# A gated linear-attention kernel with a feed-forward layer: every GpSimd operation also waits for the last VectorE operation on SBUF ahead of it in the planned order

## The chip, the cores and the metric

One NeuronCore of a Trainium2 chip runs the whole program. The metric is the device time of one execution in microseconds, lower is better. Runs of the kernel before the change: 465.85, 466.42 and 466.65 us, median 466.42.

## The reference

Two stages follow each other. First a stabilised recurrence over 768 steps, for 4 batches and 8 heads with head size 40; then a feed-forward layer whose weights are given in float64.

```python
for t in range(S):                                   # S = 768
    m_new = np.maximum(f_gate[:, :, t] + m, i_gate[:, :, t])
    f_stab = np.exp(f_gate[:, :, t] + m - m_new)
    i_stab = np.exp(i_gate[:, :, t] - m_new)
    C = f_stab * C + i_stab * outer(v_t, k_t)        # 40 x 40 for each head
    n = f_stab * n + i_stab * k_t
    y[:, :, t] = sigmoid(o_gate_t) * (C q_t) / max(abs(n q_t), 1)
x = y.transpose(0, 2, 1, 3).reshape(3072, 320)
h = x @ w_in                                         # 320 x 2048
out = (h * np.clip(h + 3, 0, 6) / 6) @ w_out         # 2048 x 320
```

## The kernel before, in words

The recurrence is cut into chunks of 64 steps. A piece of work is a pair of chunks (128 tokens) of one batch; 24 such pieces are grouped into seven units of 2, 2, 4, 4, 4, 4 and 4 pieces, and the eight heads are worked on in two groups of four ("quads").

For each piece and quad TensorE makes score, state and output products in a PSUM tile `xya` (L479, L489, L506, L512); VectorE and GpSimd mask and weigh (`gw`, L401, L406; keys in `nat`, L370) and carry the state `C` (L443, L452, L455). Per unit and quad the output `on` is gated and divided: L593, L595 and L596 make the divisor `rd`, L597 (step `o1`) multiplies by the gate, L598 (step `o2`) divides. L207 copies 64 columns of `on` to where the third transpose wants them, and L613 transposes `on` on TensorE into `xa`; L621 and L623 split that into two parts `xh` and `xl`.

The feed-forward layer runs at full precision by splitting: each weight slice comes as float64 words (`raw`), ScalarE takes the parts out (L648, L653, L658), VectorE clips, shifts and adds (L663, L664, L669, L674) to a float32 `yi` (first layer) or `vr` (second layer). A high part is cast (L207, `whi`, `vh`) and the low part is the difference (`wlo` L695 for GpSimd, `wtl` L692 and L693 on VectorE, `vl` L710). The first layer is L738 (eight matmuls of a 128-column group, tile `h`); ScalarE's L755 and VectorE's L757 make the gated `g` (`gv` in the first unit), which is split into `gh` (L207) and `gl` (L768, on GpSimd or VectorE), and L784 to L786 (L781 in the first unit) accumulate the second layer in `acc`. Output tiles are copied and stored from the SP queue.

Each step was registered with `add(key, engines, function, after, ...)`. The order of all steps on all engines is the table `ORDER`, written out beforehand: each token holds the number of a step, the letter of the engine that runs it (`d` VectorE, `g` GpSimd, `a` ScalarE, `p` TensorE, `q` the SP queue) and buffer slots. A loop at the end walks through the table and calls the step. The lists `after` serve there only for an assertion that what a step needs stands ahead of it in the table; the waits in the program are made by the tile framework, from who writes and reads which tile. Steps whose entry carries `lock=1` are those that read and write SBUF without PSUM and have some size: L274 to L286, L370, L401, L406, L597, L598, the casts L207 out of SBUF, L663 to L674, the differences L692 to L695, L710 and L768. The small divisor steps L593, L595 and L596 do not carry it.

Of the kernel before, what the change touches and what calls it, by code (L numbers as in the profile page):

```python
# [14 lines left out]
ALU = mybir.AluOpType  # L15
ET = mybir.EngineType

B, H, S, D = 4, 8, 768, 40
# [110 lines left out]
class Ops:  # L129
# [5 lines left out]
    def add(self, key, engs, fn, after=(), get=(), **meta):  # L135
        assert key not in self.at, key
        self.at[key] = len(self.ops)
        self.ops.append((key, engs, fn, list(after), list(get)))
        self.meta[key] = meta
# [3 lines left out]
def mlstm_moe_kernel(ctx: ExitStack, tc: tile.TileContext, ig, fg, qkd, natd, ond, w_in, w_out, ident_d, out, dump=None):  # L143
    nc = tc.nc
# [30 lines left out]
    tiny = cst.tile([128, 1], F32, name="tiny")  # L175
# [14 lines left out]
    T = Ops()  # L190
    add = T.add
# [8 lines left out]
    def E(c):  # L200
        return {"d": nc.vector, "g": nc.gpsimd}[c]
# [28 lines left out]
    def fill(n):  # L230
        for _ in range(n):
            nc.tensor.matmul(pw, ones[:, :128], ones[:, :512], start=True, stop=True)  # L232
# [90 lines left out]
    c0 = 0  # L323
# [246 lines left out]
    for x in NAMES:  # L570
        nm = f"{x[0]}_{x[1]}_{x[2]}"
# [5 lines left out]
    def fin(u, quad, c0, n):  # L577
        task = f"{u}_{quad}"
        nm = f"{task}_{c0}"
        W = 160 * n  # L580

        def hts():
            return V["ht", task][:, c0 : c0 + n]

        def hf():
            return hts().rearrange("p u h e -> p (u h) e")

        def ofs():
            return V["on", u][:, c0 : c0 + n, quad * 160 : quad * 160 + 160].rearrange("p u (h e) -> p u h e", h=4)

        def r1(e):
            rd = V["rd", nm] = at.tile([128, 4 * UM], F32, tag=f"rd{got[f'rd{nm}'][1]}", name=f"rd{nm}")[:, : 4 * n]
            nc.vector.scalar_tensor_tensor(rd, hf()[:, :, D], -1.0, hf()[:, :, D], ALU.mult, ALU.max)  # L593
        add(f"r1{nm}", "d", r1, [f"b2{task}_{c0 + n - 1}"], get=[(f"rd{nm}", ("rd",))], kind="tiny", n=8)
        add(f"r2{nm}", "d", lambda e: nc.vector.tensor_scalar(V["rd", nm], V["rd", nm], 1.0, 2.0, ALU.max, ALU.mult), [f"r1{nm}"], kind="tiny", n=8)  # L595
        add(f"r3{nm}", "d", lambda e: nc.vector.reciprocal(V["rd", nm], V["rd", nm]), [f"r2{nm}"], kind="recip", n=8)  # L596
        add(f"o1{nm}", "d", lambda e: nc.vector.scalar_tensor_tensor(ofs(), ofs(), 1.0, hts()[:, :, :, 0:D], ALU.add, ALU.mult), [f"b2{task}_{c0 + n - 1}", f"tanh{u}"], kind="tt", n=W, lock=1)  # L597
        add(f"o2{nm}", "dg", lambda e: E(e).tensor_tensor(ofs(), ofs(), V["rd", nm].rearrange("p (u h) -> p u h", u=n)[:, :, :, None].broadcast_to([128, n, 4, D]), ALU.mult), [f"o1{nm}", f"r3{nm}"], kind="tt", n=W, lock=1)  # L598
        T.free(f"rd{nm}", [f"o2{nm}"])
        T.free(f"ht{task}", [f"o1{nm}"])  # L600
# [25 lines left out]
    for u in range(NU):  # L626
        for quad in range(2):
            for c0, n in steps(u):
                fin(u, quad, c0, n)
        for f in range(3):  # L630
            for c0, n in steps(u):
                turn(u, f, c0, n)
        T.free(f"x{u}", [f"m1_{u}_{NF-1}"])
# [193 lines left out]
    def name(a):  # L827
        return T.alias.get(a, a)

    done = set()  # L830
    keys = list(T.at)
    for tok in ORDER.split():
        if tok[0] not in "FT":
            i = next(k for k, ch in enumerate(tok) if ch.isalpha())
            chosen[T.ops[int(tok[:i])][0]] = tok[i]
    with tc.manual_schedule(engines={ET.PE, ET.Activation, ET.DVE, ET.Pool, ET.SP}):
        for tok in ORDER.split():
            if tok[0] == "F":
                fill(int(tok[1:] or 1))
                continue  # L840
            if tok[0] == "T":
                nc.scalar.activation(pre, half, AF.Tanh)
                continue
            i = next(k for k, ch in enumerate(tok) if ch.isalpha())
            key, engs, fn, after, get = T.ops[int(tok[:i])]
            e, slots = tok[i], tok[i + 1 :].split("/") if len(tok) > i + 1 else []
            assert e in engs and key not in done and all(name(a) in done for a in after), (key, [a for a in after if name(a) not in done])
            for (who, tags), s in zip([g for g in get if g[0] not in got], slots, strict=True):
                k, n = divmod(int(s), 10)
                assert n < SLOTS[tags[k]], (key, who)  # L850
                got[who] = (tags[k], n)
            fn(e)
            done.add(key)
        assert len(done) == len(T.ops), [k for k in keys if k not in done][:9]

# [66 lines left out]
```

## Time and profile before

| | |
|---|---|
| median of three runs | 466.42 us (465.85 to 466.65) |
| the profiled execution, own time | 464.87 us |
| its span on the engines' clock | 463.2 us |
| mean granted TensorE clock | 0.996 of full speed |
| busy: TensorE, weight load | 97%, 84% of the span |
| busy: VectorE, ScalarE, GpSimd | 65%, 47%, 26% |
| chain that ended last | TensorE 85%, VectorE 9%, ScalarE 2% |

The profiled execution took 464.87 us, 1.55 us less than the median of the runs; its engines' span of 463.2 us leaves 1.67 us around it. Busy shares are means over the whole span. Stages of the program differ, so they are read by stretches of time. A row of a timeline gives start, duration, engine, line, operation and tiles; where the engine was idle ahead of it, the row ends with the idle time and what ended it.

### The profile page before, as it was taken

The page shows a single profiled execution, that of the slowest core. Times are in us where ns is not written, and L with a number is a line of the kernel's source. Part 1 is how long each engine was busy: PE and PEld are TensorE (multiplying, and loading weights), DVE is VectorE, ACT ScalarE, POOL GpSimd, SP SyncE. Part 2 cuts the span into 40 slices and gives each one's busy share as a digit, 9 for nine tenths or more (in the row PEclk, how much of TensorE's full clock was granted, in tenths as well). Part 3 has the DMA queues.
Part 4 walks back from the last instruction along what each step waited for, and adds up shares of the span by engine and source line. Part 5 has one row for each costly group of instructions (what it writes and reads, how often), then busy time and mean ns, then how long its engine had stood idle before and what let it go on. Part 6 is the DMA issues. An engine that isn't in the chain of part 4 may idle for free.

```text
span 463.2 us, 12600 instructions
## 1 busy us (share of the span) xinstructions
PE 449.1 (97%) x5243; PEld 388.3 (84%) x5249; DVE 298.8 (65%) x752; ACT 215.8 (47%) x482; POOL 122.4 (26%) x155
## 2 busy tenths in 40 slices
PE   8879989999999999999999999999999999999997
PEld 4547767899888888988889988988989898989896
DVE  6999999978866376856655763576555646443423
ACT  5788798777343434263343353243551232321231
POOL 3152225265311307502213134132112201020130
PEclk9989999999999999999999999999999999999999
DMA  6998887276304450244421442432322000010001
GB/s 208 281 315 265 234 258 203 59 176 169 94 20 119 119 151 4 78 142 121 115 77 44 131 139 60 108 102 89 101 69 78 1 1 1 16 57 1 1 1 57
DMA packets 24977, 49.38 MB, mean 107 GB/s; under 512 B 2840, under 2 KB 15960, under 8 KB 24920
## 3 DMA queue, kind: packets, MB, share of 16 engines
q1 hardware_dynamic: 24696, 47.89, 35.5%
q8 instruction: 41, 0.67, 0.6%
q10 hardware_dynamic: 224, 0.69, 0.5%
q14 instruction: 16, 0.13, 0.1%
HBM read 44.53 MB, written 4.03 MB: 105 GB/s over the span
## 4 chain that ended last, share of the span: by engine, by line
PE 85%; DVE 9%; ACT 2%; issue 1%; DMA 1%; SPq 0%; DVEq 0%; ACTq 0%
PE h L738 35%; PE acc L784 11%; PE acc L785 11%; PE acc L786 11%; PE xya L506 3%; PE xya L479 3%; PE pw L232 2%; PE xya L489 2%; PE xa L613 2%; PE xya L512 2%; PE acc L781 1%; DVE on L597 1%; DMA st<-in_qk_dram 1%; DVE on L598 1%; DVE gv L757 1%
## 5 line engine op out<-in xcount | busy, mean ns | idle before, releaser
L755 ACT ACTIVATE g<-h,half 128x512 f32<-128x512 f32 (+1 forms) x96 | 61.8, 651 | 128.3 <-PE h L738 92.9
L784 PE MATMUL acc<-vh,gh 128*128 128x320 f32 x352 | 111.5, 317 | 0.0
L757 DVE SCALAR_TENSOR_TENSOR g<-g,h 128x512 f32<-128x512 f32 (+1 forms) x96 | 61.2, 640 | 77.4 <-ACT g L755 77.3
L785 PE MATMUL acc<-vl,gh 128*128 128x320 f32 x352 | 108.6, 309 | 0.0
L786 PE MATMUL acc<-vh,gl 128*128 128x320 f32 x352 | 108.5, 308 | 0.0
L768 POOL TENSOR_TENSOR gl<-g,gh 128x512 fp32r<-128x512 f32 (+1 forms) x40 | 48.7, 1222 | 183.6 <-DVE gh L207 104.2
L738 PE MATMUL h<-xh,whi 128*128 128x512 f32 (+1 forms) x224 | 83.9, 375 | 2.4 <-DVE gv L757 1.7
L738 PE MATMUL h<-xh,wlo 128*128 128x512 f32 (+1 forms) x224 | 80.8, 361 | 0.0
L738 PE MATMUL h<-xl,whi 128*128 128x512 f32 (+1 forms) x224 | 80.5, 360 | 0.0
L784 PEld LDWEIGHTS acc<-vh,gh 128*128 128x128 f32 x352 | 66.0, 188 | 2.5
L785 PEld LDWEIGHTS acc<-vl,gh 128*128 128x128 f32 x352 | 66.1, 188 | 1.8
L786 PEld LDWEIGHTS acc<-vh,gl 128*128 128x128 f32 x352 | 66.0, 188 | 0.0
L738 PEld LDWEIGHTS h<-xh,whi 128*128 128x128 f32 x224 | 42.0, 187 | 11.4 <-DVE gv L757 3.7
L205 ACT CAST gh<-g 128x512 fp32r<-128x512 f32 (+1 forms) x53 | 30.0, 571 | 39.8 <-PE acc L785 19.5
L738 PEld LDWEIGHTS h<-xh,wlo 128*128 128x128 f32 x224 | 42.1, 188 | 6.9
L768 DVE TENSOR_TENSOR gl<-g,gh 128x512 fp32r<-128x512 f32 (+1 forms) x56 | 40.0, 722 | 12.2 <-ACT gh L205 10.9
L738 PEld LDWEIGHTS h<-xl,whi 128*128 128x128 f32 x224 | 42.1, 188 | 4.5
L738 PE MATMUL h<-xl,wtl 128*128 128x512 f32 (+1 forms) x112 | 40.5, 361 | 0.0
L738 PE MATMUL h<-xh,wtl 128*128 128x512 f32 (+1 forms) x112 | 40.2, 359 | 0.0
L419 DVE TENSOR_TENSOR gw<-xya,gw 128x256 f32<-128x256 f32 x48 | 20.0, 416 | 10.7 <-PE xya L489 7.4
L452 DVE SCALAR_TENSOR_TENSOR C<-C,dec,xya 128x42 f32<-128x42 f32 x100 | 20.6, 251 | 9.1 <-PE xya L489 9.0
L207 DVE CAST gh<-g 128x512 fp32r<-128x512 f32 (+1 forms) x43 | 19.3, 451 | 7.5 <-PE acc L785 6.1
(136 smaller groups left out, 683.2 us busy)
## 6 DMA issues: line engine op xcount, KB each, us to landing
st<-in_qk_dram SPq DMA_DIRECT2D x48, 280.0 KB, 4.2
nat<-in_nat_dram SPq DMA_DIRECT2D x48, 206.0 KB, 3.2
rawo<-in_w_out_dram SPq DMA_DIRECT2D x8, 640.0 KB, 7.9
gw<-gsc SPq DMA_DIRECT2D x20, 256.0 KB, 4.3
rawi<-in_w_in_dram SPq DMA_DIRECT2D x7, 640.0 KB, 8.5
out_dram<-ob SPq DMA_DIRECT2D x24, 160.0 KB, 3.0
on<-in_on_dram SPq DMA_DIRECT2D x5, 640.0 KB, 4.9
rawi<-in_w_in_dram ACTq DMA_DIRECT2D x1, 640.0 KB, 4.2
```

The lines of the kernel that those rows point to most:

```text
L205: nc.scalar.copy(dst, src)
L207: E(c).tensor_copy(dst, src)
L419: add(f"fr{nm}", "d", lambda e: nc.vector.tensor_tensor(V["gw", task][:, cp], V["xy", "S", nm][:, :, 0:128].rearrange("p c (j t) -> p j c ...
L452: nc.vector.scalar_tensor_tensor(Cn[:, j], cur[:, j], dc[:, j : j + 1], kv[:, hc, j], ALU.mult, ALU.add)
L479: nc.tensor.matmul(xy[h * Q : h * Q + Q, c, j * Q : j * Q + Q], st[rs, j, h], st[rs, j, 2 + (h != c)], start=True, stop=True)
L738: nc.tensor.matmul(hp[:, :n], w, x[:, :n], start=k == 0, stop=k == len(seq) - 1)
L755: nc.scalar.activation(V["g", nm], V["h", nm][:, :n], AF.Relu, bias=half, scale=1.0 / 6.0)
L757: add(f"gg{nm}", "d", lambda e: nc.vector.scalar_tensor_tensor(V["g", nm], V["g", nm], 1.0, V["h", nm][:, :n], ALU.min, ALU.mult), [f"re{n ...
L768: add(f"gl{nm}", "gd", lambda e: E(e).tensor_sub(V["gl", nm], V["g", nm], V["gh", nm].bitcast(F32)), [f"gh{nm}"], kind="tt", n=n, lock=1)
L784: nc.tensor.matmul(acc, gh[:, ts_], V["VH", f // 4][:, f % 4, :], start=f == 0, stop=False)
L785: nc.tensor.matmul(acc, gh[:, ts_], V["VL", p][:, f % 2, :], start=False, stop=False)
L786: nc.tensor.matmul(acc, gl[:, ts_], V["VH", f // 4][:, f % 4, :], start=False, stop=f == NF - 1)
```

## The change

Two things are edited. In `fin`, two lists `after` now name every step that made a part of `ht`, not only the last one. In the final loop, each GpSimd step gets one more dependency: its first GpSimd instruction also waits for the last instruction of the latest VectorE step with `lock=1` that the table has ahead of it.

```diff
-        add(f"r1{nm}", "d", r1, [f"b2{task}_{c0 + n - 1}"], ...
+        add(f"r1{nm}", "d", r1, [f"b2{task}_{c0 + i}" for i in range(n)], ...
...
+    sync = mybir.DependencyInfo(mybir.DependencyClass.Sync, mybir.DependencyReason.DATA)
+    ahead = None
     for tok in ORDER.split():
...
+            traced = nc.cur_bb.bb.instructions
+            n0 = len(traced)
             fn(e)
+            new = traced[n0:]
+            if e == "g" and ahead is not None:
+                tc.add_manual_dep(next(x for x in new if x.engine == ET.Pool), ahead.name, sync, reason="port")
+            if e == "d" and T.meta[key].get("lock"):
+                ahead = [x for x in new if x.engine == ET.DVE][-1]
             done.add(key)
```

The sequence of instructions on every engine stays as it was; what changes is what GpSimd's instructions wait for. On GpSimd, where units 0 and 1 meet (last slice of `wlo`, then `gw` of unit 2 and the first `vl`; DVE_49 counts finished VectorE instructions, the other names those of other engines and of loads):

```order
-L695 TENSOR_TENSOR wlo<-yi_862,whi 128x2x256 [waits Activation_49]
+L695 TENSOR_TENSOR wlo<-yi_862,whi 128x2x256 [waits DVE_49,Activation_49]
 L598 TENSOR_TENSOR on_1086<-on_1086,rd_0_0_858 128x2x160 [waits DVE_49,Activation_49]
-L401 TENSOR_TENSOR gw_0_1048<-gw_0_1048,mask 128x256 [waits DMAHW5_49,PE_49]
-L710 TENSOR_TENSOR vl_1169<-vr_699,vh_1139 128x640 [waits Activation_49]
+L401 TENSOR_TENSOR gw_0_1048<-gw_0_1048,mask 128x256 [waits DMAHW5_49,DVE_49,PE_49]
+L710 TENSOR_TENSOR vl_1169<-vr_699,vh_1139 128x640 [waits DVE_49,Activation_49]
```

Three of the four rows gained a wait for VectorE; the row in between had one already and now waits for a later count. GpSimd's queue has 86 instructions that only wait, where it had 73.

What some of the GpSimd operations now wait for, from the table `ORDER` (times are those of the profile before):

| GpSimd operation, its start | VectorE operation it now waits for, its end |
|---|---|
| L695 `wlo` of slice 3, 26.09 | L597 `on` of unit 0, quad 0, 27.87 |
| L207 `on` of unit 0, 31.09 | L664 `yi` of slice 4, 31.43 |
| L695 `wlo` of slice 4, 37.61 | L663 `yo` of slice 1, 42.08 |
| L695 `wlo` of slice 5, 43.58 | L693 `wtl` of slice 4, 45.30 |
| L370 `nat`, 47.24, and L275 `i_s`, 47.66 | L664 `yo` of slice 1, 49.36 |
| L695 `wlo` of slice 7, 63.98 | L664 `yo` of slice 4, 66.32 |
| L598 `on` of unit 1, quad 0, 69.73 | L664 `yo` of slice 5, 71.33 |
| L401 `gw` of unit 2, 71.11 | L598 `on` of unit 1, quad 1, 74.48 |
| L710 `vl` of slice 0, 72.38 | L401 `gw` of unit 2, 75.48 |
| L710 `vl` of slice 7, 116.61 | L598 `on` of unit 2, quad 1, 121.00 |
| L598 `on` of unit 6, quad 0, 363.07 | L768 `gl` of unit 5, 378.72 |
| L768 `gl` of unit 5, 387.75 | L598 `on` of unit 6, quad 1, 391.24 |

## Rows read from the trace of the kernel before

**Rows 1.** The page's busy times of the engines over the whole span.

```profile
PE 449.1 (97%) x5243; PEld 388.3 (84%) x5249; DVE 298.8 (65%) x752; ACT 215.8 (47%) x482; POOL 122.4 (26%) x155
```

**Rows 2.** Busy time by stretch; columns: stretch, its length, PE, PEld, DVE, ACT, POOL, clock, DMA.

```profile
24.00:34.00 10.00, 7.18 (x74) 3.41 (x74) 9.69 (x28) 8.76 (x23) 5.60 (x8) 0.84 0.99 306
34.00:50.00 16.00, 14.43 (x222) 12.13 (x221) 15.54 (x39) 13.98 (x25) 5.77 (x7) 1.00 0.82 255
50.00:76.00 26.00, 23.83 (x244) 18.33 (x245) 24.55 (x64) 21.16 (x42) 7.63 (x8) 1.00 0.84 239
130.00:350.00 220.00, 220.00 (x2705) 195.18 (x2704) 133.30 (x340) 89.16 (x205) 58.37 (x75) 1.00 0.33 95
```

**Rows 3.** The chain that ended last, pieces on VectorE and ScalarE: start, duration, what.

```profile
26.41 1.46 DVE on L597
...
38.28 0.99 DVE f_s L276
...
43.59 1.40 DVE wtl L692
...
55.25 0.69 ACT yi L648
...
72.87 1.62 DVE on L598
74.57 0.30 ACT on L205
```

**Rows 4.** Timeline of GpSimd, 26 to 79 us.

```profile
26.09 1.43 POOL L695 TENSOR_TENSOR wlo<-yi,whi 128x512 fp32r<-128x512 f32 x1 [0.70 <-ACT whi L205]
...
31.09 0.49 POOL L207 COPY on<-on 128x128 f32<-128x128 f32 x1 [1.70 <-DVE on L598]
...
43.58 1.27 POOL L695 TENSOR_TENSOR wlo<-yi,whi 128x512 fp32r<-128x512 f32 x1 [4.45 <-DVE f_s L283]
47.24 0.46 POOL L370 TENSOR_TENSOR nat<-nat,wT 128x160 f32<-128x160 f32 x1 [2.39 <-DMA nat<-in_nat_dram]
47.66 0.66 POOL L275 TENSOR_TENSOR i_s<-i_s,m_s 64x128 f32<-64x128 f32 x1
...
72.38 1.75 POOL L710 TENSOR_TENSOR vl<-vr,vh 128x640 fp32r<-128x640 f32 x1 [0.46 <-ACT vh L205]
```

**Rows 5.** Timeline of VectorE, 23 to 79 us: stretched operations and others of their kind.

```profile
29.78 0.44 DVE L597 SCALAR_TENSOR_TENSOR on<-on,ht 128x320 f32<-128x320 f32 x1
...
37.49 0.48 DVE L663 TENSOR_SCALAR yi<-yi 128x640 f32<-128x640 f32 x1
...
46.72 0.28 DVE L692 TENSOR_TENSOR wtl<-yi,wtl 64x128 fp32r<-64x128 f32 x1
...
50.01 0.27 DVE L286 TENSOR_TENSOR i_s<-i_s,f_s 64x128 f32<-64x128 f32 x1
...
64.64 1.15 DVE L663 TENSOR_SCALAR yo<-yo 128x640 f32<-128x640 f32 x1
...
66.96 0.17 DVE L593 SCALAR_TENSOR_TENSOR rd<-ht 128x8 f32<-128x8 f32 x1
```

**Rows 6.** Timelines around 121 and 392 us: VectorE first, then TensorE.

```profile
116.68 1.78 DVE L401 TENSOR_TENSOR gw<-gw,mask 128x256 f32<-128x256 f32 x1
...
388.09 1.92 DVE L597 SCALAR_TENSOR_TENSOR on<-on,ht 128x640 f32<-128x640 f32 x1
...
121.49 0.66 PE L613 MATMUL xa<-ident,on 128*128 128x128 f32 x4 [0.84 <-ACT on L205]
...
391.99 0.63 PE L613 MATMUL xa<-ident,on 128*128 128x128 f32 x4 [0.61 <-DVE g L757]
```

**Rows 7.** Timelines around 203 to 209 us (VectorE, ScalarE) and at 363 us (GpSimd).

```profile
203.38 0.69 DVE L768 TENSOR_TENSOR gl<-g,gh 128x512 fp32r<-128x512 f32 x1
...
209.47 0.69 ACT L755 ACTIVATE g<-h,half 128x512 f32<-128x512 f32 x1 [2.31 <-DVE gl L768]
...
363.07 1.31 POOL L598 TENSOR_TENSOR on<-on,rd 128x640 f32<-128x640 f32 x1 [0.40 <-DVE rd L596]
```

More of the change, by code (lines that the diff above doesn't have):

```diff
@@ L593, in r1 @@
             nc.vector.scalar_tensor_tensor(rd, hf()[:, :, D], -1.0, hf()[:, :, D], ALU.mult, ALU.max)
-        add(f"r1{nm}", "d", r1, [f"b2{task}_{c0 + n - 1}"], get=[(f"rd{nm}", ("rd",))], kind="tiny", n=8)
+        add(f"r1{nm}", "d", r1, [f"b2{task}_{c0 + i}" for i in range(n)], get=[(f"rd{nm}", ("rd",))], kind="tiny", n=8)
         add(f"r2{nm}", "d", lambda e: nc.vector.tensor_scalar(V["rd", nm], V["rd", nm], 1.0, 2.0, ALU.max, ALU.mult), [f"r1{nm}"], kind="tiny", n=8)
         add(f"r3{nm}", "d", lambda e: nc.vector.reciprocal(V["rd", nm], V["rd", nm]), [f"r2{nm}"], kind="recip", n=8)
-        add(f"o1{nm}", "d", lambda e: nc.vector.scalar_tensor_tensor(ofs(), ofs(), 1.0, hts()[:, :, :, 0:D], ALU.add, ALU.mult), [f"b2{task}_{c0 + n - 1}", f"tanh{u}"], kind="tt", n=W, lock=1)
+        add(f"o1{nm}", "d", lambda e: nc.vector.scalar_tensor_tensor(ofs(), ofs(), 1.0, hts()[:, :, :, 0:D], ALU.add, ALU.mult), [f"b2{task}_{c0 + i}" for i in range(n)] + [f"tanh{u}"], kind="tt", n=W, lock=1)
         add(f"o2{nm}", "dg", lambda e: E(e).tensor_tensor(ofs(), ofs(), V["rd", nm].rearrange("p (u h) -> p u h", u=n)[:, :, :, None].broadcast_to([128, n, 4, D]), ALU.mult), [f"o1{nm}", f"r3{nm}"], kind="tt", n=W, lock=1)
```

## The prediction

> **What bounds the kernel now.** The page's busy times come first [rows 1]: TensorE is busy for 97% of the span, VectorE for 65%, GpSimd for 26%. By these alone nothing that GpSimd does could matter. So the stretches are read next [rows 2]. From 130 to 350 us TensorE is busy all the time. From 24 to 76 us it is not: there VectorE is busy for 49.8 of 52 us, TensorE for 45.4, because the float64 weights of the feed-forward layer are being prepared while the first units already run. The chain of waits says the same [rows 3]: in that stretch it runs mostly along VectorE, with ScalarE in between around 55 to 60 us. Whatever VectorE loses there moves everything behind it.
>
> The reader should now see what VectorE loses. On the chain stand single operations that are far too long for their size. L597 at 26.41 takes 1.46 us, and the same instruction at 29.78 takes 0.44 [rows 3, 5]. It stood beside a GpSimd subtraction from 26.09 to 27.52 [rows 4], and it ended 0.35 us behind that one's end. So it was not slowed down in proportion, it stood still until GpSimd had finished. L692 at 43.59 (1.40 us, elsewhere 0.28) meets the GpSimd row at 43.58, L598 at 72.87 (1.62 us, where L597 of the same size takes 0.44) the one at 72.38, in the same way [rows 3 to 5]. The long ones are operations on SBUF alone. I read it as a lock: of a GpSimd operation and a VectorE operation on SBUF, the later one stands still.
>
> **The change, part by part.** The two lists in `fin` feed an assertion and cost nothing; no instruction moves. The 13 further wait instructions on GpSimd sit on an engine that idles three quarters of the time [rows 1]; between back-to-back GpSimd rows with a wait there lies under 0.1 us, and I take zero. What is left is the wait itself. It removes the case in which GpSimd is early, starts ahead of a VectorE operation that the table has ahead of it, and holds that one up. I took each GpSimd start and the end of the VectorE operation that it will wait for: of some 140 operations, about 60 start before that end, most by 0.3 to 6 us. These will be held. The others stay.
>
> *Stalls on the chain that go, 24 to 76 us.* Each is the duration less that of its kind alone. At 26.41: 1.46 - 0.44 = 1.0 us. At 38.28 (L276, alone like L286 of its size): 0.99 - 0.27 = 0.7. At 43.59: 1.40 - 0.28 = 1.1. At 64.64: 1.15 - 0.48 = 0.7. At 72.87: 1.62 - 0.44, or 1.1 with a little off for its second full input [rows 3, 5]. Together 4.6 us. In each case the GpSimd operation that held the lock is one that will now wait for this very operation or a later one.
>
> *What of it reaches TensorE.* Not all, since something else is late next.
> - First part, to 34 us. The 1.0 us at 26.41 hardly survives: the third transpose of unit 0 needs the GpSimd copy at 31.09 [rows 4], and this will wait for L664 `yi`, which ended at 31.43, 0.3 us later. The delayed `wlo` will also run into a divisor step of the second quad. I take 0.1 us.
> - Second part, to 50 us. 0.7 + 1.1 = 1.8 us, from which about 0.1 goes back. Then VectorE's L286 at 50.01 needs `i_s` of GpSimd [rows 4, 5]. That chain begins at 47.24 with a load that had just landed, and it won't start sooner. From there: 47.24 + 0.46 + 0.66 gives 48.4, against 50.01. So the gain is capped at 1.6 us here, and I take 1.6 for both parts together (bounds: 0.6, if the load path slips by another microsecond, since the DMA engines are 82 to 99% busy there; 1.8 without the cap).
> - Third part, to 76 us. Around 55 to 60 us ScalarE leads, and keeps what was gained. The 0.7 at 64.64 is mostly given back: `wlo` of slice 7 (about 1.3 us) now begins behind L664 at 66.32 and meets L593 at 66.96, which is 0.17 us long [rows 5]; it will stand for some 0.6. The 1.1 us at 72.87 ended in 0.9 us of idle time on ScalarE ahead of its copy at 74.57 [rows 3]; but ScalarE's own work on the last slice of unit 0 ends only shortly before that. I take 0.4 us (bounds 0 and 1.1).
>
> Sum up to 76 us: 2.0 us (bounds 0.6 and 2.9). Behind that TensorE is dense, and a microsecond gained at 76 us is one at the end.
>
> *Two late stalls.* L401 at 116.68 stood behind the `vl` subtraction of 116.61 and took 1.78 us, for 256 elements where L597 needs 0.44 us for 320; some 1.4 us go. It stood ahead of the last division of unit 2, and TensorE's transpose at 121.49 had idled 0.84 us for that [rows 6]. The `vl` will wait until 121.0 less the gain; its user comes later. Gain 0.8 us, limited by the idle time. L597 at 388.09 took 1.92 us for 640 elements, twice those of the row with 0.44; TensorE idled 0.61 us for its result at 391.99 [rows 6]. Gain 0.6.
>
> *Costs.* The held operations delay their users. The longest: `on` of unit 6 moves from 363.07 to about 378.7; its user is the transpose at 391.99, so some 12 us of cover are left [rows 6, 7]. A state update near 192 us must wait for L768 of 203.38, and four operations queue behind it; they take some 2 us, and ScalarE waits for the last of them, but it idles 2.31 us ahead of 209.47 [rows 7]. `vl` of slice 7 is needed by second-layer matmuls behind the transpose of 121.49. If such a cover were gone, the cost would be up to 2 us, the length of the queued operations. I take zero for them, as the transpose copy is in the first part already.
>
> Sum: 2.0 + 0.8 + 0.6 = 3.4 us less. The profiled execution took 464.87 us, so by its own time 461.5 us. The median of the runs is 1.55 us higher; from it, 466.42 - 3.4 = 463.0 us.
>
> **The rivals.**
>
> *A, the early gain is lost to loads (0.20).* From 24 to 76 us the DMA engines are 82 to 99% busy [rows 2], and one load shows as a cap above. If the weights land no sooner, VectorE will wait for them instead of for GpSimd, and only the late terms of 1.4 us stay: 466.42 - 1.4 = 465.0 us. Against it: VectorE idles only 2.2 us of 52 in that stretch [rows 2], so loads were mostly there in time.
>
> *B, no change (0.11).* The stalls reappear elsewhere by as much as they vanish, and the waits turn out mostly met: 466.4 us. For it: some 80 of the 140 waits are met anyway.
>
> *C, slower (0.09).* The wait moves GpSimd to exactly the end of one VectorE operation on SBUF, where the next such operation may follow. Then GpSimd is first again and holds up the next one, and to this the waits are added. Place and price: the copy at 31.09 costs 0.4 us; `i_s` would begin at 49.4 + 0.5, end at 50.6 and hold L286 by 0.6 us [rows 4, 5]. With no stall saved, 466.42 + 1.0 = 467.4 us. It decides by the gap between the end that is waited for and the next VectorE operation on SBUF, against about 1.3 us of GpSimd work. Two cases from the rows: behind 45.30 the next one is at 46.72, far enough; behind 66.32 it is at 66.96, too near, and I counted that one as given back [rows 5]. VectorE's many operations on PSUM stand between the others, so I take the first case for the commoner one. The Trainium skill, "SBUF — State Buffer", section "Who interferes with whom", states that whoever issues first has the shared ports for the whole instruction and the other fully blocks, and that issue order decides who that is. The trace agrees that the later one stands still (1.46 us instead of 0.44); by that rule alone the wait only chooses a new loser each time, which is this rival, at 467.4 us.
>
> **How the numbers follow.** My forecast has 0.60, with 461.0 to 464.6 us as its own range: the bounds of the early term (0.6 to 2.9) give 464.4 to 462.1, and the profiled execution's own time, less 3.4, is 461.5; a little more where stalls off the chain vanish too. A adds 464.2 to 465.5. B and C, 0.20 together, are left out above. So the range is 461.0 to 465.6 us. A measurement of this kernel can tell about 0.2% from no change, which is 0.93 us, so faster means below 465.5: forecast and A, 0.80, less a little for A's upper end, 0.79. Same: B and the rest, 0.12. Slower: 0.09.
>
> **What would show it.** Right: L597 near 26.4 takes about 0.45 us, L692 near 43 0.28, L598 near 71 0.48, L401 near 115 0.42, L597 near 385 0.8; TensorE's idle time ahead of the transposes near 119 and 389 is gone; GpSimd's `wlo` of slice 4 starts about 4 us later; `i_s` on GpSimd still begins near 47.7. VectorE's small steps L593 or L595 near 28 and 65 are longer than now. Wrong: the same lengths on VectorE in other places of the chain (C), new idle time of VectorE or ScalarE that ends with a load (A), or TensorE idle behind 130 us with GpSimd named as the releaser.

## The result and the profile after

The kernel with the change took 461.44 us (median of six runs, 460.44 to 463.83), the kernel before 466.38 us in the same comparison (six runs, 464.57 to 466.65). The ratio is 0.9907, with a 95% interval of 0.988 to 0.9934; on 466.4 us that is 4.3 us less (3.1 to 5.6). A second measurement of the same program gave 461.19 us and a ratio of 0.9903 (0.9876 to 0.9929). Forecast were 463.0 us and 3.4 us less: the direction holds, the size was a little too small, and the time lies in the stated range.

The profiled execution of the change took 461.8 us, with a span of 460.1. First the busy times and the chain's shares by engine, from its page; the rows of before are [rows 1].

```profile
PE 449.9 (98%) x5249; PEld 389.3 (85%) x5249; DVE 288.6 (63%) x752; ACT 215.2 (47%) x482; POOL 116.6 (25%) x155
...
PE 93%; DVE 3%; DMA 1%; ACT 1%; issue 0%; SPq 0%
```

The same instructions keep VectorE busy 10.2 us less (298.8 to 288.6) and GpSimd 5.8 us less (122.4 to 116.6): part of both had been standing, which the profile counts as busy (L597, for one, was busy for 1.46 us and is now for 0.49). VectorE's part of the chain that ended last went from 9% to 3%; TensorE has 93% of it, not 85%.

Busy time by stretch, columns as in [rows 2]:

```profile
34.00:50.00 16.00, 15.35 (x229) 12.89 (x230) 15.56 (x46) 15.63 (x30) 5.55 (x8) 1.00 0.86 256
50.00:76.00 26.00, 24.62 (x253) 19.31 (x252) 24.12 (x65) 22.86 (x48) 7.29 (x8) 1.00 0.89 248
```

TensorE is busy for more of each early stretch (from 34 to 76 us 39.97 us instead of 38.26), and in the dense part (130 to 350 us) all of the time, as before. The stretch from 24 to 34 us can't be compared: here a load let TensorE wait until 23.65, so that everything stood about 3 us later at 26 us, and the granted clock of that stretch was 0.68 instead of 0.84. Both profiles have that wait, of different length; first before, then after (timeline of TensorE):

```profile
21.80 0.52 PE L479 MATMUL xya<-st 40*64 40x64 f32 x13 [0.77 <-DMA st<-in_qk_dram]
```

```profile
23.65 0.88 PE L479 MATMUL xya<-st 40*64 40x64 f32 x13 [2.70 <-DMA st<-in_qk_dram]
```

So the two profiles can't be subtracted from the start on. They can from one instruction of VectorE to another. The named operations, from VectorE's timeline of the change; those of before are [rows 3, 5, 6]:

```profile
29.40 0.49 DVE L597 SCALAR_TENSOR_TENSOR on<-on,ht 128x320 f32<-128x320 f32 x1
...
45.39 0.29 DVE L692 TENSOR_TENSOR wtl<-yi,wtl 64x128 fp32r<-64x128 f32 x1
...
48.43 0.49 DVE L664 TENSOR_SCALAR yo<-yo 128x640 uint32<-128x640 uint32 x1
...
49.91 0.28 DVE L286 TENSOR_TENSOR i_s<-i_s,f_s 64x128 f32<-64x128 f32 x1
...
62.13 1.10 DVE L595 TENSOR_SCALAR rd<-rd 128x8 f32<-128x8 f32 x1
...
66.42 0.83 DVE L593 SCALAR_TENSOR_TENSOR rd<-ht 128x8 f32<-128x8 f32 x1
...
72.74 0.49 DVE L598 TENSOR_TENSOR on<-on,rd 128x320 f32<-128x320 f32 x1
...
73.83 0.55 DVE L401 TENSOR_TENSOR gw<-gw,mask 128x256 f32<-128x256 f32 x1
...
115.57 0.42 DVE L401 TENSOR_TENSOR gw<-gw,mask 128x256 f32<-128x256 f32 x1
...
385.83 0.82 DVE L597 SCALAR_TENSOR_TENSOR on<-on,ht 128x640 f32<-128x640 f32 x1
```

L597 has gone from 1.46 to 0.49 us, L692 from 1.40 to 0.29, L598 from 1.62 to 0.49, L401 from 1.78 to 0.42 and the late L597 from 1.92 to 0.82. Of the stalls on the prediction's list, L276 (0.99 us, [rows 3]) is down to 0.42, and L663 near 64.7 from 1.15 to 0.49 us. L593 at 66.42 has become longer, 0.83 instead of 0.17: the place where the prediction gave most back. The two transposes that had idled ahead, [rows 6], now follow the matmuls without a wait (timeline of TensorE):

```profile
119.40 0.60 PE L613 MATMUL xa<-ident,on 128*128 128x128 f32 x4
...
388.95 0.60 PE L613 MATMUL xa<-ident,on 128*128 128x128 f32 x4
```

GpSimd's timeline of the change, beside [rows 4]:

```profile
43.77 1.31 POOL L695 TENSOR_TENSOR wlo<-yi,whi 128x512 fp32r<-128x512 f32 x1 [3.03 <-DVE yo L663]
...
49.05 0.46 POOL L370 TENSOR_TENSOR nat<-nat,wT 128x160 f32<-128x160 f32 x1 [1.62 <-PE xya L489]
49.47 0.41 POOL L275 TENSOR_TENSOR i_s<-i_s,m_s 64x128 f32<-64x128 f32 x1
...
74.53 1.56 POOL L710 TENSOR_TENSOR vl<-vr,vh 128x640 fp32r<-128x640 f32 x1 [0.42 <-DVE gw L401]
```

They begin where a VectorE operation ends. (The row of L370 names TensorE, but it begins 0.13 us behind the end of L664 at 48.92, which it now waits for.) Most are shorter, too: `wlo` takes 1.29 to 1.31 us where it took up to 1.52, and `i_s` (L275) 0.41 instead of 0.66.

### The profile page after: what moved, and what is told of

The parts are those of the page before. It is cut to its first block, busy times and chain, and to the rows that moved or that the text cites. A ratio compares the mean times of both kernels' runs of the same rounds, so it can differ in the third digit from the quotient of the medians.

```text
span 460.1 us, 12619 instructions
## 1 busy us (share of the span) xinstructions
PE 449.9 (98%) x5249; PEld 389.3 (85%) x5249; DVE 288.6 (63%) x752; ACT 215.2 (47%) x482; POOL 116.6 (25%) x155
## 4 chain that ended last, share of the span: by engine, by line
PE 93%; DVE 3%; DMA 1%; ACT 1%; issue 0%; SPq 0%
PE h L738 38%; PE acc L784 12%; PE acc L785 11%; PE acc L786 11%; PE xya L506 3%; PE xya L479 3%; PE acc L781 3%; PE pw L232 2%; PE xya L489 2%; PE xya L512 2%; PE xa L613 2%; DMA st<-in_qk_dram 1%; PE gb L381 1%; PE pc L301 0%; PE gb L384 0%; DVE vr L669 0%
## 5 line engine op out<-in xcount | busy, mean ns | idle before, releaser
L738 PE MATMUL h<-xh,whi 128*128 128x512 f32 (+1 forms) x224 | 83.9, 374 | 0.9 <-ACT dec L319 0.6
L768 POOL TENSOR_TENSOR gl<-g,gh 128x512 fp32r<-128x512 f32 (+1 forms) x40 | 47.0, 1179 | 145.9 <-DVE gh L207 57.6
L738 PE MATMUL h<-xh,wlo 128*128 128x512 f32 (+1 forms) x224 | 80.8, 361 | 0.0
L738 PE MATMUL h<-xl,whi 128*128 128x512 f32 (+1 forms) x224 | 80.5, 359 | 0.0
L738 PEld LDWEIGHTS h<-xh,whi 128*128 128x128 f32 x224 | 42.0, 187 | 9.3 <-DVE gv L757 1.4
L738 PEld LDWEIGHTS h<-xh,wlo 128*128 128x128 f32 x224 | 42.0, 188 | 6.8
L768 DVE TENSOR_TENSOR gl<-g,gh 128x512 fp32r<-128x512 f32 (+1 forms) x56 | 38.9, 704 | 12.9 <-ACT gh L205 11.8
L738 PEld LDWEIGHTS h<-xl,whi 128*128 128x128 f32 x224 | 42.1, 188 | 4.6
L738 PE MATMUL h<-xl,wtl 128*128 128x512 f32 (+1 forms) x112 | 40.5, 361 | 0.0
L738 PE MATMUL h<-xh,wtl 128*128 128x512 f32 (+1 forms) x112 | 40.1, 358 | 0.0
L443 POOL TENSOR_TENSOR C<-C,dec 128x84 f32<-128x84 f32 x30 | 9.9, 333 | 70.3 <-DVE gl L768 38.0
L419 DVE TENSOR_TENSOR gw<-xya,gw 128x256 f32<-128x256 f32 x48 | 20.0, 416 | 11.0 <-PE xya L489 7.8
```

What stands on the lines that cost most here:

```text
L419: add(f"fr{nm}", "d", lambda e: nc.vector.tensor_tensor(V["gw", task][:, cp], V["xy", "S", nm][:, :, 0:128].rearrange("p c (j t) -> p j c ...
L738: nc.tensor.matmul(hp[:, :n], w, x[:, :n], start=k == 0, stop=k == len(seq) - 1)
L768: add(f"gl{nm}", "gd", lambda e: E(e).tensor_sub(V["gl", nm], V["g", nm], V["gh", nm].bitcast(F32)), [f"gh{nm}"], kind="tt", n=n, lock=1)
```

## The experiments

Theory, called the stall theory: while a GpSimd operation that came early runs, VectorE's next operation on SBUF stands still; the added wait takes away GpSimd's being early. Against it stand: loads that bound the early stretch anyway (prediction A), stalls that only move (C), and the thought that any delay, or any common order of the two engines, would do the same.

To compare profiles that start at different times, the table takes the time from the start of one VectorE instruction to that of another, from each run's VectorE timeline. **a**: L597 of unit 0, quad 0 (26.41 before) to L286 (50.01). **b**: on to L401 of unit 2 (75.07). **c**: on to the L455 that starts at 116.29. **d**: on to the L455 at 125.65, round the `vl` of slice 7. **e**: L597 at 388.09 to L623 at 393.27. Each row is one profile, so a to e have a scatter of their own; where its cause is known, it stands below the table.

| run | median, us | ratio to before, 95% interval | L597 at | a | b | c | d | e |
|---|---|---|---|---|---|---|---|---|
| before | 465.5 to 466.4 | 1 | 26.41 | 23.60 | 25.06 | 41.23 | 9.36 | 5.18 |
| the change | 461.44 | 0.9907 (0.988 to 0.9934) | 29.40 | 20.51 | 23.92 | 41.36 | 8.59 | 4.37 |
| again | 461.19 | 0.9903 (0.9876 to 0.9929) | 28.87 | 21.59 | 23.90 | 41.30 | 8.59 | 4.37 |
| early | 463.19 | 0.9944 (0.9919 to 0.997) | 26.18 | 23.83 | 23.92 | 42.11 | 9.34 | 5.17 |
| late | 464.26 | 0.9973 (0.9945 to 1.0001) | 26.49 | 23.50 | 25.52 | 41.84 | 8.59 | 4.38 |
| two | 464.2 | 0.9956 (0.9928 to 0.9984) | 25.34 | 23.05 | 25.07 | 41.23 | 8.31 | 4.38 |
| prev | 462.49 | 0.9931 (0.9905 to 0.9957) | 26.60 | 21.76 | 23.83 | 41.96 | 9.37 | 4.99 |
| reverse | 468.0 | 1.0053 (1.0028 to 1.0078) | 29.43 | 23.55 | 25.57 | 41.86 | 9.34 | 5.18 |
| every | 476.38 | 1.0227 (1.0191 to 1.0264) | 29.62 | 22.12 | 24.01 | 50.02 | 8.83 | 4.37 |
| small | 467.64 | 1.0032 (1.0003 to 1.0061) | 28.18 | 21.10 | 24.18 | 46.64 | 8.59 | 4.37 |
| onemore | 466.25 | 1.0008 (0.9982 to 1.0033) | 27.05 | 22.24 | 23.92 | 46.65 | 8.59 | 4.38 |
| small2 | 461.63 | 0.9914 (0.9891 to 0.9937) | 29.17 | 21.42 | 23.97 | 41.93 | 8.59 | 4.38 |
| vl2_before | 468.66 | 1.0051 (1.0023 to 1.008) | 29.29 | 23.02 | 25.53 | 41.23 | 11.19 | 5.18 |
| vl2_after | 462.28 | 0.9925 (0.9902 to 0.9947) | 26.89 | 21.45 | 23.92 | 41.98 | 8.79 | 4.37 |

Three things to know of the columns. First, `reverse` and `vl2_before` have the first stall just ahead of L597, on L692 (0.94 and 1.32 us), so it isn't in their a; their a is as long as that of the profiles that have it inside, so this stall hardly reached anything further on. Second, the runs without early waits have two values of b: 25.1 where the subtraction of slice 7 holds up L663 (by 0.66 us), 25.5 where it holds up L693 just ahead (by 1.1 us in `late`, `reverse` and `vl2_before`). Third, c has 41.2 to 41.4 us or 41.8 to 42.1 (but for `every`, `small` and `onemore`). In `late`, `small2` and `vl2_after` L593 near 100 us stands 1.6 us for a `vl`, and TensorE then idles 0.53 to 0.55 us for L419; in the change L593 takes 0.19 us, the next one on SBUF (L401, 1.14 us) stands instead, and TensorE doesn't wait. There some tenths decide whom the lock hits.

**Early and late apart.** The wait only where a counter of GpSimd steps allows it:

```diff
+    steps = 0
...
+            steps += e == "g"
-            if e == "g" and ahead is not None:
+            if e == "g" and ahead is not None and steps <= 26:
```

(`late` has `steps > 26`.)

> The added wait only for the first 26 GpSimd steps of the order, those of the first 76 us. Stall theory (VectorE stands still while a GpSimd operation that came early runs, and the wait removes that): what the whole change gained, some 4.9 us between the medians, less the two late stalls, which the trace of the change shows as 1.0 us near 121 us and 0.9 us near 390 us. So 466.4 - 3.0 = 463.4 us, with L597 near 26 to 29 us at 0.49 us, L692 near 45 at 0.29, L598 near 73 at 0.49, and L401 near 115 still at 1.8. Rival, loads (the early stretch waits for loads whatever GpSimd does, and only the late stalls count): 466.4 within 0.5 us.

> The added wait only for the GpSimd steps behind the first 26, from 76 us on. Stall theory: L401 near 116 takes 0.42 us, L597 near 388 0.82 us, TensorE no longer idles ahead of the transposes that follow them; 466.4 - 1.9 = 464.5 us, and the gains of the early and the late part add up to that of the whole. Rival, loads: all of the gain is here, 461.5 us. Second rival, waits that cost (each of the 117 waits delays GpSimd's users a little): no gain or slower, 466.4 us or above.

Measured: 463.19 us and 464.26 us, by the ratios 2.6 and 1.3 us less, together 3.9 against 4.3 to 4.5 for both at once. They add up within the intervals. The rival by which loads bound the early stretch falls: `early` alone is faster, and `late` is far from the 461.5 us of a gain that lies there alone. By its own interval, which just reaches 1, `late` could be no gain at all; that the late part counts is shown by d and e and by the next run. The table shows the two parts without the scatter of the start: `early` has the short b and the long d and e, `late` the reverse.

The early profile does not show the gain in a. TensorE stood at 40.41 for something the profile doesn't name, and the granted clock was 0.72 in the mean from 39 to 42 us (timeline):

```profile
40.41 0.37 PE L738 MATMUL h<-xl,whi 128*128 128x256 f32 x1 [1.42 <-issue]
```

So a is 23.83, though its VectorE stalls are gone (L597 0.49, L692 0.29). What held TensorE there isn't settled.

**Two waits alone.**

```diff
-            if e == "g" and ahead is not None:
+            if key in ("vl7", "gl5_12"):
```

> Only two GpSimd operations get the added wait: the subtraction vl of slice 7 (L710 near 117 us) and gl of unit 5, slice 12 (L768 near 388 us). Stall theory: both late gains by themselves, 0.8 to 1.0 us and 0.6 to 0.9 us, so 466.4 - 1.7 = 464.7 us, the same as with all waits from 76 us on. If the late gain is spread over many small stalls instead, this one gives less than half of it: 465.6 us or more.

Measured 464.2 us, 2.05 us less by the ratio, as much as `late` with its 117 waits. In its table row d and e are as short as with all of them (8.31 and 4.38). The late gain is two stalls, and no sum of many.

**One operation too early.** The wait on the last but one instead of the last:

```diff
-                ahead = [x for x in new if x.engine == ET.DVE][-1]
+                ahead, older = older, [x for x in new if x.engine == ET.DVE][-1]
```

> Every GpSimd step waits for the last but one VectorE operation on SBUF ahead of it in the order, not the last: as many waits, GpSimd held nearly as often (37 of 143 starts in the trace of before lie ahead of that end, 62 for the last one). Stall theory: GpSimd now begins just as the last one begins or ahead of it, and holds it up. wlo of slice 3 is released at 26.38, L597 starts at 26.41; wlo of slice 5 at 43.56, L692 at 43.59; wlo of slice 7 at 64.27, L663 at 64.64; vl of slice 7 at 119.97, L598 at 120.17; gl near 390 at 390.02, L598 at 390.42. So the stalls stand, on these, with the old lengths of 1.1 to 1.9 us on VectorE, and the time is 465 to 467 us. Rival, any delay of GpSimd does it (loads, memory traffic or GpSimd's own stretched operations are what it relieves): 461.5 to 463 us as for the whole change.

(For `wlo` of slice 7 the text names the wrong step: the last but one there is L663, which ended at 65.79, and L664 began at 65.83.) Measured 462.49 us, 3.2 us less. That is below the stall theory's 465 to 467, and the numbers alone would suit the rival. The timelines tell them apart, place by place. Near 26 us nothing is decided (VectorE, ScalarE and GpSimd):

```profile
26.60 0.49 DVE L597 SCALAR_TENSOR_TENSOR on<-on,ht 128x320 f32<-128x320 f32 x1
...
26.45 0.60 ACT L205 CAST whi<-yi 128x512 fp32r<-128x512 f32 x1
...
27.13 1.29 POOL L695 TENSOR_TENSOR wlo<-yi,whi 128x512 fp32r<-128x512 f32 x1 [1.55 <-DVE on L597]
```

The row of `wlo` names L597, but the subtraction needs ScalarE's `whi`, which ended at 27.05 in this profile, and it began 0.08 us later. In the kernel before it also began 0.08 us behind `whi` (26.01 and 26.09); there `whi` came ahead of L597. So L597 was spared here because `whi` was late and not by the wait, and the same holds for L692 at 43.69 (`whi` ended at 43.91, `wlo` began at 43.99). Near 63.5 us `whi` had long been there, and the end of L663 at 63.49 freed both engines (VectorE, then GpSimd):

```profile
63.01 0.48 DVE L663 TENSOR_SCALAR yo<-yo 128x640 f32<-128x640 f32 x1
63.52 0.49 DVE L664 TENSOR_SCALAR yo<-yo 128x640 uint32<-128x640 uint32 x1
...
63.63 1.54 POOL L695 TENSOR_TENSOR wlo<-yi,whi 128x512 fp32r<-128x512 f32 x1 [2.18 <-DVE yo L663]
```

VectorE's next operation was there 0.03 us later, GpSimd's 0.14 us, and it was GpSimd's that stood: 1.54 us instead of 1.29. This tie went to VectorE. Near 72, 116 and 387 us VectorE's next `lock=1` operation came later, behind small steps or operations on PSUM:

```profile
72.19 1.38 DVE L401 TENSOR_TENSOR gw<-gw,mask 128x256 f32<-128x256 f32 x1
...
115.65 0.82 DVE L597 SCALAR_TENSOR_TENSOR on<-on,ht 128x640 f32<-128x640 f32 x1
...
116.66 2.21 DVE L598 TENSOR_TENSOR on<-on,rd 128x640 f32<-128x640 f32 x1
...
116.61 1.58 POOL L710 TENSOR_TENSOR vl<-vr,vh 128x640 fp32r<-128x640 f32 x1 [4.91 <-DVE on L597]
...
119.36 0.66 PE L613 MATMUL xa<-ident,on 128*128 128x128 f32 x4 [0.84 <-ACT on L205]
...
387.13 1.74 DVE L598 TENSOR_TENSOR on<-on,rd 128x640 f32<-128x640 f32 x1
```

At 116.61 GpSimd began 0.14 us behind the end of L597, L598 another 0.05 us later, and it stood: 2.21 instead of 0.82 us. L401, freed by the change, was free here too, and yet TensorE idles the same 0.84 us as before: the stall moved from one to the next. In the table d and e are about as long as without any wait (9.37; 4.99). At 72.19 L401 stands for a `vl` that began 0.14 us behind the end of L598 (1.38 instead of 0.41 us); b ends where that row begins and doesn't show it, c is 41.96. So the exact operation matters where the next one on SBUF follows with a gap (0.19 us at 116.66, 0.40 at 387.13, 0.59 at 72.19), and where VectorE follows at once (0.03 us) it doesn't. That is rival C of the prediction, seen at work in three places. The gain of `prev` is no argument for the rival: in its a and b stalls are missing, twice by a late `whi`, once by the tie, and once (L276, 0.28 us) since the step waited for comes later than the one spared.

The Trainium skill, "SBUF — State Buffer", section "Who interferes with whom", says that issue order decides who blocks, not the shape of the operations. These rows agree (0.49 us for L664, which came 0.11 us ahead of the subtraction; 2.21 us instead of 0.82 for L598, which came 0.05 us late); what the runs add is which of two engines freed by the same end is the first.

**The wait turned round.**

```diff
-            if e == "g" and ahead is not None:
+            if e == "d" and T.meta[key].get("lock") and ahead is not None:
```

(with `ahead` the last GpSimd instruction, and the wait on the step's first VectorE instruction)

> The wait turned round: each VectorE step on SBUF waits for the last GpSimd step ahead of it in the order, and GpSimd for nothing new. Both engines then also run these steps in the order of the table at every point, but GpSimd may still be early. Stall theory: the stalls stay at their old places and lengths (L597 near 26 us 1.46, L692 near 43 us 1.40, L598 near 73 us 1.6, L401 near 117 us 1.78, L597 near 388 us 1.9), and by the trace of before 15 VectorE operations would be held besides, by 14 us in all, most of them behind 90 us where TensorE is dense: 466.4 us, up to 1 us more. Rival (keeping the two engines in the order of the table is what helps, whichever waits): 461.5 to 463 us.

Measured 468.0 us, 2.5 us slower (1.3 to 3.6). The rival falls: a common order doesn't help if VectorE is the one that gives way. The stalls stand at four of the five places with their old lengths (1.42, 1.60, 1.78, 1.92); near 29 us it was L692 that met the GpSimd subtraction (0.94 us), not L597. The cost is above the expected 0 to 1 us and wasn't located: b and c are 1.1 us longer than before, but `late` has the same b and c, so this much is also seen without the turned wait.

**Waiting for more.** First for every VectorE step, then for those on SBUF and the three small divisor steps.

```diff
-            if e == "d" and T.meta[key].get("lock"):
+            if e == "d" and any(x.engine == ET.DVE for x in new):
```

```diff
-            if e == "d" and T.meta[key].get("lock"):
+            if e == "d" and (T.meta[key].get("lock") or key[:2] in ("r1", "r2", "r3")):
```

> GpSimd steps wait for the last VectorE step of any kind ahead of them, those on PSUM and the small divisor steps too (97 of 143 starts in the trace of before would be held, 282 us in all, against 62 and 183 us). Stall theory: the stalls that the change removes stay removed, and L595 near 62 us, which stands behind wlo of slice 6 in the trace of the change (1.10 instead of 0.17), is freed too; the longer holds are covered, as GpSimd idles three quarters of the time: 460.5 to 461.5 us. Rival (holding GpSimd longer than the port needs makes its users late): 463 us or more, with TensorE or VectorE idle behind a GpSimd operation.

> As the change, but the small divisor steps L593, L595 and L596 count as steps on SBUF too, so GpSimd also waits for those that stand ahead of it. In the trace of the change L595 at 62.13 takes 1.10 us beside the GpSimd subtraction of 61.91; it lies on the chain that ended last. Stall theory: it takes 0.17 us, VectorE is 0.9 us earlier there, and the time is 461.4 - 0.9 = 460.5 us; L593 near 66.4 stays at 0.83, since it stands behind its GpSimd operation in the table. Rival (TensorE has become the bound by then): 461.4 us within 0.4.

Both expectations were wrong, and by much: 476.38 us and 467.64 us. In `small` a and b are short as in the change; c has 46.64 us instead of 41.3. I took GpSimd's idle time for cover. Two runs tell what happened there.

> The change and one VectorE step more that counts: L593 of unit 2, quad 0 (near 99.5 us). In the program only the GpSimd steps between it and the next step on SBUF of VectorE are touched: the mask step L401 near 97 us now waits for it, and gl and two vl stand behind that in GpSimd's queue. In the run where all small steps count, L401 was held from 96.3 to 99.57, TensorE stood 3.14 us for vl at 102.70, and the granted clock was 0.86 from 90 to 104 us. Queue theory: this one wait is the whole loss of that run: 461.3 + 6.4 less about 0.5 that the freed L595 near 62 us gave, so 466.5 to 468 us. Rival (the loss is the sum of many held operations): 462 to 463 us.

> The change, with L595 and L596 counting as steps on SBUF too, but not L593. Near 62 us wlo of slice 6 then waits for L595 (0.17 instead of 1.10 us), as in the run where all small steps counted; there the stall moved on to L692 at 62.41, which took 1.27 instead of 0.28. Stall theory: nothing is won there, since the next VectorE operation on SBUF follows 0.5 us behind the end that is waited for and GpSimd needs 1.3: 461.3 us within 0.6. Rival (the freed 0.9 us reaches the end): 460.4 us. If the wait on L595 near 102 us is what cost 6 us there, not the one on L593: 466 us or more.

```diff
-            if e == "d" and T.meta[key].get("lock"):
+            if e == "d" and (T.meta[key].get("lock") or key == "r12_0_0"):
```

(`small2` has `key[:2] in ("r2", "r3")` instead.) The one wait costs it all: `onemore` took 466.25 us, 4.7 us above the change by the ratios, and its c is 46.65. GpSimd and TensorE in it:

```profile
99.14 0.72 POOL L401 TENSOR_TENSOR gw<-gw,mask 128x256 f32<-128x256 f32 x1 [3.10 <-DVE rd L593]
99.83 0.90 POOL L768 TENSOR_TENSOR gl<-g,gh 128x256 fp32r<-128x256 f32 x1
100.69 3.28 POOL L710 TENSOR_TENSOR vl<-vr,vh 128x640 fp32r<-128x640 f32 x2
...
102.28 0.64 PE L785 MATMUL acc<-vl,gh 128*128 128x320 f32 x1 [3.13 <-POOL vl L710]
```

In the change the mask step had run at 96.65. Here `gl` and two `vl` stand behind it in GpSimd's queue, held up with it, and TensorE stood 3.13 us for the first `vl`. Then TensorE ran at the lower of its two levels (1.2 GHz; the granted clock from 90 to 104 us is 0.86 in the mean), as the spacing of its matmuls in the chain shows, 0.27 us at first and 0.15 us later. From `small`, where the same wait sits:

```profile
103.34 0.27 PE acc L786
...
110.33 0.15 PE acc L784
```

`small2` took 461.63 us, as the change. Its reason, VectorE and GpSimd near 63 us:

```profile
62.80 0.17 DVE L595 TENSOR_SCALAR rd<-rd 128x8 f32<-128x8 f32 x1
...
63.52 1.27 DVE L692 TENSOR_TENSOR wtl<-yi,wtl 64x128 fp32r<-64x128 f32 x1
...
63.35 1.29 POOL L695 TENSOR_TENSOR wlo<-yi,whi 128x512 fp32r<-128x512 f32 x1 [0.72 <-ACT gv L755]
```

L595 is freed (0.17 for 1.10 us), and L692 stands in its place (1.27 for 0.29). (The step that `wlo` waits for is L596 rather than L595, as the text has it: it ended at 63.20, 0.15 us ahead of `wlo` and 0.32 us ahead of L692.) Rival C again, and b is the change's, 23.97 against 23.92. `every` holds the wait of `onemore` too (GpSimd's L401 at 103.35 behind L593) and many more; its loss of 8.7 us in c wasn't taken apart further.

**The stall made longer.** `vl` of slice 7 done twice, in the kernel before and in the change (lines behind 709 count one more there).

```diff
-            E(e).tensor_sub(V["VL", i], w(), hi().bitcast(F32))
+            for _ in range(2 if i == 7 else 1):
+                E(e).tensor_sub(V["VL", i], w(), hi().bitcast(F32))
```

> The kernel before, in which the GpSimd subtraction vl of slice 7 (L710, 1.57 us near 116.6) is done twice, with the same result; no wait added. Stall theory: L401, which begins just behind the first of the two, stands until both have run, 1.78 + 1.57 = 3.35 us instead of 1.78, the transpose near 121 us comes 1.5 us later, and the time is 1.5 us above that of before. Rival (L401 is slowed in proportion, or takes its turn between two GpSimd operations): L401 stays below 2.5 us, and the time is within 0.5 us of before.

> The same doubling in the kernel with the change. Both subtractions now run behind L598 of unit 2, from about 119.1 to 122.2 us. Stall theory: L401 keeps its 0.42 us; GpSimd's gl of 120.66 moves to 122.2 and is ready at 123.0, where TensorE wants it at 122.26, so the cost is 0.7 us, from 461.3 to 462.0 us, half of what it costs without the wait. Rival (what VectorE is spared is paid in full by GpSimd's users): 1.5 us here too, 462.8 us or more.

Without the wait it took 468.66 us, 2.4 us more than before (1.1 to 3.7); with it 462.28 us, 0.9 us more than the change by the ratios. The same 1.57 us of extra GpSimd work seems to cost more than twice as much where it could get ahead of VectorE. The intervals of these two costs overlap; the profiles bear the difference out. How it costs was not as I wrote. VectorE's and GpSimd's timelines of `vl2_before`:

```profile
119.47 1.78 DVE L401 TENSOR_TENSOR gw<-gw,mask 128x256 f32<-128x256 f32 x1
121.18 1.55 DVE L593 SCALAR_TENSOR_TENSOR rd<-ht 128x16 f32<-128x16 f32 x1
...
119.40 3.29 POOL L711 TENSOR_TENSOR vl<-vr,vh 128x640 fp32r<-128x640 f32 x2 [2.78 <-ACT vh L205]
```

L401 didn't stand for both. It stood for the first, ran between the two, and the next operation of VectorE, L593, stood for the second: 1.55 us instead of 0.18. So what the two engines share was free between the two subtractions, as the rival's words "takes its turn" have it. The length expected for L401 (3.35 us) was wrong; the sum of the two stalls, 1.4 us for L401 and 1.4 for L593, is near the 2.9 expected. d grew by 1.83 us, and the transpose had idled 2.21 us instead of 0.84 (TensorE's timeline):

```profile
125.65 0.66 PE L613 MATMUL xa<-ident,on 128*128 128x128 f32 x4 [2.21 <-ACT on L205]
```

Behind that idle time the granted clock was 0.56 in the mean from 128 to 131 us. From this transpose to the first L739 of 512 columns TensorE took 5.45 us; in the kernel before (L738 there) 3.92. In `vl2_after` L401 keeps its 0.42 us, and the cost lies in the delayed `gl`, on TensorE; first `vl2_after`, then the change, whose transpose is shown above at 119.40:

```profile
118.45 0.60 PE L613 MATMUL xa<-ident,on 128*128 128x128 f32 x4
...
123.47 0.40 PE L739 MATMUL h<-xh,whi 128*128 128x512 f32 x1
```

```profile
123.26 0.39 PE L738 MATMUL h<-xh,whi 128*128 128x512 f32 x1
```

That is 5.02 us against 3.86: 1.16 us lost, more than the 0.7 I worked out, though the only idle time that the profile names in it is 0.28 us. In `vl2_before` the longer idle time and the 5.45 us make 2.9 us together. (That execution took 470.5 us, 1.8 us above its median, so the 2.9 is at the upper end.) Both amounts are higher than the 1.5 and 0.7 us expected, and the wait takes off about half, as expected.

**The change once more.** Only the label of the wait differs in its text.

> The whole change once more, for its time beside the others and for a second profile. Stall theory: 461.4 us within 0.6, with the same lengths on VectorE (0.49, 0.29, 0.49, 0.42, 0.82 at the five places named in the prediction) even if the loads of the first 25 us come at other times; in the first profile the load that frees L479 let TensorE idle 2.70 us at 23.65, and this should be seen to vary between profiles of one program. Rival (the wait itself delays the first loads): L479 near 23.6 us again.

461.19 us, the lengths as in the first profile. It also started late (L479 at 23.30, idle 2.72), so this pair alone would let the rival stand that the wait delays the loads. The other profiles decide it. Two kernels that add no wait to GpSimd started as late (L597 at 29.43 in `reverse`, 29.29 in `vl2_before`), and four with GpSimd waits that early didn't (26.18 `early`, 26.60 `prev`, 26.89 `vl2_after`, 27.05 `onemore`). The start differs from execution to execution by up to 4 us.

None of the variants beats the change by more than the scatter.

## Why the prediction was right, and where its sum was off

*What bounds, and the lock.* Right. VectorE's 10.2 us of lost busy time were standing time. The five places named have the lengths forecast, to within 0.05 us. At the first of them the wait isn't needed in every execution: L597 has 0.49 us in `reverse` and `vl2_before` as well, where the subtraction hit L692 instead. That it is freed by the wait shows in `early`, `onemore` and `vl2_after`, which start about as early as before and where `whi` came ahead of L597.

*Up to 50 us (taken at 1.6 us, bounds 0.6 to 1.8).* About right. In the five profiles without early waits (before, `late`, `two`, `reverse`, `vl2_before`) a is 23.3 us in the mean, in five with all of the change's early waits (the change, `again`, `onemore`, `small2`, `vl2_after`) 21.4: 1.9 us less (1.5 if the profile of `early`, 23.83, is counted in). The copy of `on` costs as it was said: it waits for L664, and TensorE's third transpose idles 0.32 us for it at 34.80. The cap was put in the wrong place. `i_s` did not stay near 47.7: it begins at 49.47, since L664, which its predecessor waits for, ends at 48.92. (Rival C had it begin at 49.9.) It costs little all the same: it takes 0.41 us instead of 0.66 and ends at 49.88, and L286 follows 0.03 us later, 0.3 us behind the start of L207 ahead of it, where before that was 0.16. L664 at 47.97, now 0.49 us long, was missing from my list of stalls. VectorE's timeline of the kernel before, this one and another that I passed over:

```profile
47.97 1.39 DVE L664 TENSOR_SCALAR yo<-yo 128x640 uint32<-128x640 uint32 x1
...
70.43 0.90 DVE L664 TENSOR_SCALAR yo<-yo 128x640 uint32<-128x640 uint32 x1
```

*Up to 76 us (taken at 0.4 us, bounds 0 and 1.1).* This is the step that failed. b is 25.35 us in the mean without the waits and 23.9 with them, within 0.07 us in the five profiles: 1.4 us, above the upper bound. Against the profile of before alone, on which the forecast was worked out, it is 1.1 us, the bound itself; where L693 was the one held up, 1.6. Either way the 0.4 us was too small by a factor of three. What I gave back was right: 0.66 us gained on L663 at 64.64, 0.66 lost on L593 at 66.42. But I took off most of the 1.1 us at 72.87, since ScalarE's own work would end only shortly before its copy. It hardly bound; ScalarE before, then in the change:

```profile
74.57 0.30 ACT L205 COPY on<-on 128x128 f32<-128x128 f32 x1 [0.90 <-DVE on L598]
```

```profile
73.02 0.36 ACT L621 CAST xh<-xa 128x256 fp32r<-128x256 f32 x1
73.32 0.30 ACT L205 COPY on<-on 128x128 f32<-128x128 f32 x1
```

The copy comes at 73.32, right behind both L598 (which ended at 73.23) and ScalarE's own L621, and without the 0.90 us of idle time ahead of it. From L286 on, that is 1.15 us earlier than before. Besides, L664 at 70.43 had stood for 0.4 us (0.90, now 0.49).

*The two late stalls (0.8 and 0.6 us).* d is 0.77 us shorter, e 0.81 us. The gain at the first was larger than d shows: d ends at a VectorE step that now waits 0.20 us for GpSimd's held L443, and by TensorE, from the start of d to the first L738 of 512 columns (125.41 before, 123.26 in the change), 1.04 us were won. I had bounded both by the idle time ahead of the transposes, 0.84 and 0.61 us. That was no bound. Near 392 us: from L597 (2.26 us earlier than before) to the transpose (391.99 to 388.95, 3.04 us earlier) 0.78 us were won, more than the idle time shown, as the ends of matmuls in a profile are modelled.

*Costs at nothing.* Right for the change, whose timeline names no idle time of TensorE from 76 us on, and narrow. `onemore` shows that a wait on a step one place further, ahead of the same queue, costs 4.7 us. That such a price exists was in the prediction ("up to 2 us, the length of the queued operations") and was set too low: 3.13 us of idle time, and a lower clock behind it.

*Rivals.* A falls: with the early waits alone 2.6 us of the gain are there. B falls by the interval. C doesn't decide the change, but it is real: the stalls of `prev` and `small2` moved on to the next operation, as it says, where the gap was 0.19 to 0.59 us and GpSimd's operation 1.3 to 1.6.

By stretches the gain is 1.9 (a) + 1.4 (b) + 1.0 (d, by TensorE) + 0.8 (e), 5.1 us, where the runs gave 4.3 (3.1 to 5.6). The forecast's 3.4 us was low in two terms, 0.4 us for the third part and 1.4 for the two late stalls.

## What to carry to other kernels

A VectorE operation on SBUF that takes 1 to 2 us where its like takes 0.4, and ends just behind a GpSimd operation, has stood still for it; if it lies on the path, let GpSimd wait for the operation that it would hold up, and pick that one by what VectorE does next: nothing on SBUF should follow within GpSimd's duration unless it follows at once (0.03 us here). Before a wait is added, look at the queue behind the waiting instruction, not at how much the engine idles: one wait too many cost as much as all the others together had won. When two profiles start differently, compare from one instruction to another. And before a stall that is missing is put down to an edit, look whether everything else that the waiting operation needs came when it used to: in `prev` the row of `wlo` named L597, and it was `whi` that was late.

## What was not expected of the hardware

- When one VectorE operation's end frees both engines, VectorE's next one starts 0.03 us later if nothing lies between, GpSimd's 0.14 us (`prev`, 63.63 and 116.61): the tie went to VectorE at 63.52, and with a gap of 0.19 us to GpSimd at 116.61.
- Between two GpSimd operations that follow each other directly VectorE can get in: in `vl2_before` it stood 1.4 us for the first, ran one operation, and stood 1.4 us for the second.
- Even an operation of 8 elements per partition stands for the rest of the GpSimd operation: L595 at 62.13 took 1.10 us instead of 0.17, until the subtraction of 61.91 had ended.
